# Attention, top-1 experts and a dense softplus layer on one core: the dense layers' rows made gapless in the order of the expert phases, loaded early, and scattered by token at the end

## The chip, the cores and the metric

The kernel runs on one core of a Trainium2 chip. The metric is the device time of one execution in microseconds (us); less is better. Before the change the median of three runs is 951.3 us (951.3, 952.59 and 945.84).

## What is computed

Three layers stand behind one another, all in float32. The reference, cut to what matters:

```python
scores = scale * np.matmul(q, k.transpose(0, 1, 3, 2))          # 4 x 8 x 576 x 576, head size 64
cum = np.cumsum(np.log(np.clip(f, 0.0001, 1.0)), axis=-1)
scores = np.where(causal, -1000000000.0, scores + cum[:, :, :, None] - cum[:, :, None, :])
x = softmax(scores) @ v                                         # as 2304 tokens x 512

expert_idx = np.argmax(logits, axis=1)                          # normed x times normed expert_emb, over tau
gate_w = probs[np.arange(N), expert_idx]                        # softmax over 8 experts
for e in range(E):
    mask = expert_idx == e
    h = np.maximum(x[mask] @ w1[e], 0.0)                        # 512 -> 1024
    out[mask] = gate_w[mask, None] * (h @ w2[e])                # 1024 -> 512

h = x @ w_in                                                    # 512 -> 2048, x is the out above
g = np.maximum(h, 0.0) + np.log1p(np.exp(-np.abs(h)))
return g @ w_out                                                # 2048 -> 512
```

## The kernel before

Float32 products are made of two parts each, a high one (names with h: `xh`, `wh`, `yth`, `gh`) and a low one (`xl`, `wl`, `ytl`, `gl`), and three matmuls: high by high, high by low and low by high. A weight is split by ACT (the high part) and DVE (the difference); both lines are L969 and L970 for the experts' weights and L1251 and L1252 for the dense ones.

The attention fills the first 240 us. It writes x to DRAM (`xd`). Then `route` sorts the tokens by expert into slots of 128 rows; `gidx` holds the token of each row of a slot, `sidx` the row of `yd` to which the result goes: before the change that is the token itself, and for an empty row of a slot a place behind the 2304 real rows.

**Experts.** Nine phases run in the order `ORDER`, each with one expert's weights: phases of kind t take 3 slots, of kind b 2, of kind s 1 (21 slots in all). A phase has four steps that matter here.
- `xgather` (L990): POOL gathers the rows of the phase after the next one from `xd` by `gidx`, one indirect DMA for each slot, into the three buffers `xg`. `xprep` (L1006 to L1008) transposes them on PE and splits them on ACT and DVE.
- The first matmul (L1049) makes h; ACT and DVE take the relu and split it (L1054, L1055). In the one phase of kind s (`small`, phase 6) the operands change places (L1089): ACT writes the relu to `hs` (L1093), PE transposes it (L1099), ACT and DVE split it (L1102, L1103).
- `l2` (L1029) makes y in eight rounds of fb; with three slots a round has 9 matmuls. In the last phase the loop over slots is outside the loop over fb, so the three slots are done one after another.
- `scatter`: ACT evicts y (L1013), and POOL scatters it to `yd` by `sidx` (L1020). y has three buffers.

The loads of raw weights stand on SP. `gates` (L845 to L854) makes the gate of each token behind phase 0. `turn_gates` (L861, L867) turns the gates with two transposes on PE inside the second matmul of phase 1, so that they stand by token in `g.gate`.

**The branch.** Behind the phases a branch (`tc.If(over > 0)`, L1174) jumps over the work for tokens that found no place in the 21 slots. In the profiled execution it jumps. Every engine goes through it.

**Dense layers** (`ffn`). The 18 tiles of 128 rows are taken in five chunks of 4, 3, 4, 3 and 4 tiles. At the start SP loads the four tiles of chunk 0 from `yd` (L1289), DVE multiplies each row by its gate (L1299), PE transposes (L1303), ACT and DVE split (L1304, L1305). For later chunks POOL does the multiplication, and the rest is spread over the units of the chunk before. Each chunk has 16 units of 128 columns of the 2048. Unit n goes through three stations: `l1` on PE (L1316); the softplus, whose parts are ACT's Abs, Exp and two copies (L1325 to L1328) and Ln (L1335), one operation on POOL (L1329), two on DVE (L1340, L1341), and the split into `gh` (ACT, L1344) and `gl` (DVE, L1346); and `l2` (L1358), which PE does three units later. Behind the last unit of a chunk ACT and DVE evict the tiles to `ob` (L1363), and SP stores them to the output (L1365).

The order on each engine is that in which the code issues the instructions; a wait on a semaphore stands ahead of an instruction where its data or its buffer comes from another engine. Instructions behind a waiting one on the same engine wait too. Software DMA queues (DMASW) are those that POOL writes, hardware ones (DMAHW) those of SP and ACT; there are eight semaphores of each.

## Time and profile before

| What | Value |
|---|---|
| median of three runs | 951.3 us |
| lowest, highest | 945.84, 952.59 us |
| profiled execution | 946.24 us |
| its span, from the first to the last instruction | 944.5 us |
| PE busy | 881.7 us (93%), 6294 matmuls |
| DVE, ACT, POOL busy | 618.1, 604.8, 347.0 us |
| mean granted clock of PE | 0.978 |
| share of PE in the chain of waits | 74% |
| DMA | 109.39 MB, mean 116 GB/s |

The profile is of one execution. Its timeline lists instructions by engine with their start and duration; in brackets stands how long the engine was idle before one, and what ended that (for example a DVE instruction of line L864). The chain of waits starts from the last instruction and goes back, at each step to what released it. A duration of a matmul covers its whole way through the pipeline; in a stream the next one starts 0.23 us later.

### The profile page before, as it was taken

Reading aid. Unit: us, or ns where it says so; the run is one execution under the profiler, and the core shown is the slowest. Engines: PE = TensorE matmul, PEld = TensorE weight load, DVE = VectorE, ACT = ScalarE, POOL = GpSimd, SP = SyncE. Lnnn points to the kernel's source line nnn. Section 1 sums busy time; section 2 is a strip of 40 time slices with the busy share of each in tenths; the row PEclk is TensorE's granted clock in tenths of the full one; section 3 lists DMA queues with packets and bytes.
Section 4 is the critical chain, followed back from the end, with each engine's and each line's share of the span. In section 5 each row is a group of like instructions: output and inputs, shape, how many; then the busy total and the mean of one; then the engine's idle time right before and its main releaser. Section 6 shows DMA issues by size and latency. Waiting matters only on the chain.

```text
span 944.5 us, 17382 instructions
## 1 busy us (share of the span) xinstructions
PE 881.7 (93%) x6294; PEld 755.2 (80%) x6294; DVE 618.1 (65%) x1327; ACT 604.8 (64%) x1139; POOL 347.0 (37%) x474
## 2 busy tenths in 40 slices
PE   3999999999299999999999599999999999999998
PEld 2788887878288898897988488889988888988886
DVE  4888888888765777776768476455555455455544
ACT  4778878886624555545444398667676666767664
POOL 6777876774322122122010075323222322222221
PEclk9999999999589999999999799999999999999999
DMA  8766666660337878778853200011001001000001
GB/s 182 177 157 149 163 150 146 166 187 28 113 122 241 300 243 276 231 264 282 281 208 128 82 0 12 12 43 37 23 13 45 11 1 57 23 1 34 1 1 44
DMA packets 103007, 109.39 MB, mean 116 GB/s; under 512 B 62264, under 2 KB 71480, under 8 KB 102912
## 3 DMA queue, kind: packets, MB, share of 16 engines
q1 hardware_dynamic: 99296, 97.02, 35.2%
q0 software_dynamic: 3360, 11.01, 3.3%
q8 instruction: 51, 0.84, 0.4%
q14 instruction: 44, 0.36, 0.1%
q10 hardware_dynamic: 256, 0.16, 0.1%
HBM read 93.15 MB, written 15.02 MB: 115 GB/s over the span
## 4 chain that ended last, share of the span: by engine, by line
PE 74%; DMA 8%; issue 6%; ACT 5%; DVE 5%; POOL 2%; SPq 0%; ACTq 0%; DVEq 0%; POOLq 0%
PE h L1316 21%; PE o L1358 21%; PE h L1049 7%; PE y L1029 5%; DMA yd<-y,sidx 4%; PE s L268 4%; PE av L391 2%; DMA raw<-in_moe_w_dram 2%; PE pt L339 2%; DVE wl L970 2%; PE tps L195 1%; PE av L392 1%; PE av L393 1%; PE s L274 1%; PE s L270 1%
## 5 line engine op out<-in xcount | busy, mean ns | idle before, releaser
L1346 DVE TENSOR_TENSOR gl<-e,gh 128x512 fp32r<-128x512 f32 (+1 forms) x80 | 97.7, 1221 | 170.5 <-ACT gh L1344 170.5
L1329 POOL TENSOR_TENSOR e<-u,e 128x512 f32<-128x512 f32 (+1 forms) x80 | 94.6, 1182 | 281.6 <-ACT u L1328 278.1
L1316 PE MATMUL h<-yth,dl 128*128 128x512 f32 (+1 forms) x320 | 117.9, 369 | 0.0
L1358 PE MATMUL o<-dl,gh 128*128 128x512 f32 x288 | 112.5, 391 | 0.0
L1325 ACT ACTIVATE e<-h 128x512 f32<-128x512 f32 (+1 forms) x80 | 44.4, 554 | 104.0 <-PE h L1316 78.9
L969 ACT ACTIVATE wh<-raw 128x1024 fp32r<-128x1024 f32 x64 | 66.9, 1057 | 49.4 <-DMA raw<-in_moe_w_dram 44.3
L970 DVE TENSOR_TENSOR wl<-raw,wh 128x1024 fp32r<-128x1024 f32 x64 | 77.5, 1221 | 23.4 <-ACT wh L969 22.9
L1049 PE MATMUL h<-xh,wh 128*128 128x384 f32 (+1 forms) x256 | 80.5, 314 | 1.9 <-DVE hl L1055 1.5
L1049 PE MATMUL h<-xh,wl 128*128 128x384 f32 (+1 forms) x256 | 79.6, 311 | 1.5 <-DVE wl L970 1.5
L1049 PE MATMUL h<-xl,wh 128*128 128x384 f32 (+1 forms) x256 | 79.7, 311 | 0.0
L319 DVE SCALAR_TENSOR_TENSOR pts<-pt,pts 128x512 f16<-128x512 f32 (+3 forms) x128 | 69.7, 567 | 11.9 <-ACT pts L316 11.2
L1020 POOL DMA_INDIRECT yd<-y,sidx x21 | 22.2, 1056 | 141.3 <-ACT y L1013 138.2
L316 ACT ACTIVATE pts<-pt 128x512 f16<-128x512 f32 (+3 forms) x128 | 58.4, 495 | 22.1 <-PE pt L329 10.7
L293 ACT ACTIVATE p<-sm,mx 128x512 f32<-128x512 f32 (+3 forms) x128 | 67.8, 558 | 0.0
L1029 PE MATMUL y<-wh,hh 128*128 128x512 f32 x168 | 67.1, 399 | 0.0
L1316 PEld LDWEIGHTS h<-yth,dl 128*128 128x128 f32 x320 | 60.1, 188 | 7.6
L1029 PE MATMUL y<-wl,hh 128*128 128x512 f32 x168 | 66.0, 393 | 0.0
L1341 DVE TENSOR_TENSOR e<-e,v 128x512 f32<-128x512 f32 (+1 forms) x80 | 59.7, 747 | 7.3
L290 DVE CUSTOM_DVE_ANT_0 sm<-s,cb 128x512 f32<-128x512 f32 (+3 forms) x128 | 58.3, 484 | 8.0 <-PE s L270 7.1
L1358 PEld LDWEIGHTS o<-dl,gh 128*128 128x128 f32 x288 | 54.1, 188 | 10.3
L1316 PE MATMUL h<-yth,wh 128*128 128x512 f32 (+1 forms) x160 | 60.4, 378 | 0.7 <-ACT yth L1304 0.7
L391 PE MATMUL av<-vp,pts 128*128 128x65 f16 (+2 forms) x480 | 59.2, 197 | 0.5 <-DVE vbits L240 0.5
(301 smaller groups left out, 2557.2 us busy)
## 6 DMA issues: line engine op xcount, KB each, us to landing
raw<-in_moe_w_dram SPq DMA_DIRECT2D x68, 512.0 KB
cb<-ncum SPq DMA_DIRECT2D x32, 288.0 KB
raw<-in_moe_w_in_dram SPq DMA_DIRECT2D x16, 512.0 KB
raw<-in_moe_w_out_dram SPq DMA_DIRECT2D x16, 512.0 KB
cb<-ncum SPq DMA_DIRECT2D x32, 144.0 KB
out_dram<-ob SPq DMA_DIRECT2D x18, 256.0 KB
qt<-in_q_dram SPq DMA_DIRECT2D x32, 128.0 KB
kt<-in_k_dram SPq DMA_DIRECT2D x32, 128.0 KB
```

Of the source, the lines that this page charges most:

```text
L293: nc.scalar.activation(p[:, 0:n], s[:, 0:n], ACTF.Exp, scale=-1.0, bias=m)
L319: nc.vector.scalar_tensor_tensor(lo, ps, UP, hi, op0=ALU.mult, op1=ALU.subtract)
L391: nc.tensor.matmul(o, ph, vp[0:kk, j, h, 0:D + 1], start=(j == 0), stop=False)
L969: nc.scalar.activation(hi, r, ACTF.Copy)
L970: nc.vector.tensor_sub(lo, r, hi.bitcast(F32))
L1029: nc.tensor.matmul(py[a], x[:, 128 * a:128 * a + 128], w[:, fb % 2], start=(fb == 0 and m == 0 and w is wh), stop=(fb == 7 and m == 1))
L1049: nc.tensor.matmul(pl, x[:, fs], y[:, c], start=(c == 0 and m == 0), stop=(c == 3 and m == 2))
L1316: nc.tensor.matmul(pl, w[:, fs], x[:, d], start=(d == 0 and m == 0), stop=(d == 3 and m == 2))
L1329: nc.gpsimd.tensor_sub(e, u, e)
L1341: nc.vector.tensor_add(d, d, u)
L1346: nc.vector.tensor_sub(gl, d, gh.bitcast(F32))
L1358: nc.tensor.matmul(PO[c][a], x, w, start=(fb == 0 and m == 0 and w is wh), stop=(fb == FB - 1 and m == 1))
```

## The change

**Rows.** `sidx` no longer holds the token. A new `compact` counts, slot by slot in the order of the phases, how many rows of each partition are taken (one matmul with ones, a scan on DVE), and gives the taken rows of `yd` numbers without gaps. So the first 512 rows are results of the first phases. The token travels with the row: `yd` has 528 columns in place of 512, and POOL copies the token's number into the last 16 before the scatter.

**Gates.** `gates` moves into phase 0, behind its first relu. `turn_gates` goes. `store_gates` writes the gates to DRAM (`gd`), POOL gathers them for each slot (`ggather`, 21 more indirect DMAs of one value per row) and the eviction of y multiplies by them (L1078, a scale per row).

**Early load.** In the last phase four tiles are loaded (`rows.load`), transposed and split in rounds fb 2 to 5 (`rows.prep`); the loop over slots is now inside, so that the three scatters come together at the end. The first load is preceded by one of a single element that waits for the scatters issued until then.

**Dense layers.** They keep the pools `xg` and `y` and the PSUM banks of the experts. The multiplication by the gate goes. The first two splits of the second dense weights, which stood ahead of the loop, move into units 0 and 1. The output goes out by POOL, scattered by the token (`oidx`). In the small phase `hs` takes a buffer of the pool `y`.

```diff
-    V.tensor_scalar(pv[:, 0], pid[:, 0], -1.0, 1.0, op0=ALU.mult, op1=ALU.add)
-    V.tensor_tensor(pv[:, 0], pv[:, 0], g.dmf, op=ALU.mult)
-    V.tensor_tensor(g.sidx, g.gidx, pv[:, 0], op=ALU.add)
+    x = 0
+    while x < NMAIN:
...
+        V.tensor_copy(g.flag[:, x:x + y], pid[:, 0, m:m + y])
+        x += y
...
+def store_gates(tc, g, p, ps):
+    nc = tc.nc
+    t = ps()
+    nc.tensor.transpose(t[0:T, 0:128], g.gs, g.ident)
+    turned = p.tile([T, 128], F32, name="turned", bufs=1)
+    nc.vector.tensor_copy(turned, t[0:T, 0:128])
+    nc.scalar.dma_start(g.gd.rearrange("(t p) o -> t (p o)", p=128), turned)
+
+def compact(tc, g, p, ps):
...
+    ones = p.tile([128, 128], BF16, name="ones", bufs=1)
+    nc.gpsimd.memset(ones, 1.0)
+    n = ps()[:, 0:NMAIN]
+    nc.tensor.matmul(n, ones, g.flag, start=True, stop=True)
     yield
+    sums = p.tile([128, NMAIN], F32, name="sums", bufs=1)
+    V.tensor_tensor_scan(sums, ones[:, 0:NMAIN], n, 0.0, op0=ALU.mult, op1=ALU.add)
+    V.tensor_copy(g.total, sums[:, NMAIN - 1:NMAIN])
+    V.tensor_tensor(sums, sums, n, op=ALU.subtract)
+    V.tensor_scalar(sums, sums, g.row, None, op0=ALU.add)
+    V.tensor_tensor(sums, sums, g.dmf, op=ALU.subtract)
+    V.tensor_tensor(sums, sums, g.flag, op=ALU.mult)
+    V.tensor_tensor(g.sidx, sums, g.dmf, op=ALU.add)
+    a = p.tile([128, NMAIN], I32, name="batch", bufs=1)
+    gate_rows(V, g.grow, g.gidx, a)
+    V.tensor_copy(g.tok, g.gidx)
...
+        def ggather(ph):
+            for s in slots(ph):
+                nc.gpsimd.indirect_dma_start(out=g.gsl[:, s:s + 1], out_offset=None, in_=g.gd,
+                                             in_offset=bass.IndirectOffsetOnAxis(ap=g.grow[:, s:s + 1], axis=0))
...
         def scatter(ph, a, py):
-            y = yp.tile([128, DM], F32, name="y", tag="y")
-            nc.scalar.activation(y, py, ACTF.Copy)
...
+            y = yp.tile([128, WROW], F32, name="y", tag="y")
+            nc.gpsimd.tensor_copy(y[:, DM:WROW], tok.to_broadcast([128, WROW - DM]))
+            nc.scalar.activation(y[:, 0:DM], py, ACTF.Copy, scale=gate)
...
+            if last:
+                for a in range(SIZES[0]):
+                    rows.load(0, a)
+            if ph == 0:
+                store_gates(tc, g, hp, bank)
...
-                if ph == 1 and i in (5, 6):
-                    next(turned, None)
...
+                if fb == 1:
+                    ggather(ph)
...
-                if last and i % 3 == 1:
-                    conv.split("i", i // 6, i // 3 % 2)
-                if fb == 7:
-                    for a in rows:
-                        scatter(ph, a, py[a])
+                if last:
+                    conv.split("i", fb // 2, fb % 2)
+                    if 2 <= fb < 2 + SIZES[0]:
+                        rows.prep(0, fb - 2, bank)
+            for a in range(w):
+                scatter(ph, a, py[a])
...
-                hs = hp.tile([128, 512], F32, name="hs", tag="hs", bufs=2)
+                hs = yp.tile([128, WROW], F32, name="hs", tag="y")[:, 0:DM]
...
+    def load(self, c, a):
+        g, t = self.g, FIRST[c] + a
+        y = self.y[t] = g.xp.tile([128, WROW], F32, name="yg", tag="xg", bufs=3)
+        if t == 0:
+            self.nc.sync.dma_start(y[0:1, 0:1], g.yd[0:1, 0:1])
+        self.nc.sync.dma_start(y, (g.yd if c else g.ydv[NSLOT])[128 * t:128 * t + 128])
+
+    def prep(self, c, a, bank):
...
+        nc.gpsimd.tensor_copy(g.oidx[:, t:t + 1], y[:, DM:DM + 1])
+        p = bank().rearrange("p (d n) -> p d n", n=128)
+        for d in range(4):
+            nc.tensor.transpose(p[:, d], y[:, 128 * d:128 * d + 128], g.ident)
+        nc.scalar.activation(hi[:, :, a], p, ACTF.Copy)
+        nc.vector.tensor_sub(lo[:, :, a], p, hi[:, :, a].bitcast(F32))
...
-                    r = 128 * (FIRST[c] + a)
-                    nc.sync.dma_start(out[r:r + 128, :], o)
+                    t = FIRST[c] + a
+                    nc.gpsimd.indirect_dma_start(out=outv[t], out_offset=bass.IndirectOffsetOnAxis(ap=g.oidx[:, t:t + 1], axis=0),
+                                                 in_=o, in_offset=None)
...
-        for a in range(SIZES[0]):
-            yload(0, a)
-        for pair in range(2):
-            conv.split("o", 0, pair)
-        late = iter([(q, pair) for q in range(1, 4) for pair in range(2)])
...
+        late = iter([(q, pair) for q in range(4) for pair in range(2)])
...
-                        conv.split("o", q, pair, nc.gpsimd)
+            for q, pair in [next(late, (0, None))]:
+                if pair is not None:
+                    conv.split("o", q, pair, nc.gpsimd if q else nc.vector)
```

The order of the program shows three places. The first is ACT behind the branch, before: the two splits of dense weights, the four splits of transposed rows, and unit 0's softplus up to `gh`, the high part of its result.

```order
L1174 UNCONDITIONAL_BRANCH [waits Activation_49,Activation_sequencer_49]
L1251 ACTIVATE wh<-dw 128x1024 [waits DVE_49,PE_49,Activation_49]
L1251 ACTIVATE wl<-dw 128x1024
L1304 ACTIVATE yth_12338<-yt 128x4x128 [waits PE_49] x4
L1325 ACTIVATE e<-h 128x512 [waits DMASW4_49,DMASW2_49,DMASW6_49,DMASW0_49,PE_49]
L1326 ACTIVATE e<-e 128x512 [waits Activation_49]
L1327 ACTIVATE u<-e 128x512 [waits DMASW2_49,DMASW1_49,DMASW6_49,DMASW0_49,Activation_49]
L1328 ACTIVATE u<-u 128x512 [waits Activation_49]
L1335 ACTIVATE v<-u 128x512 [waits Activation_49]
```

And the same place after the change (the lines have moved: L1396 is Abs, L1351 the split of weights, L1415 the copy to `gh`).

```order
L1396 ACTIVATE e<-h 128x512 [waits DMASW5_49,DMASW6_49,DMASW4_49,DMASW7_49,DMASW3_49,DMAHW0_49,DMASW1_49,DMAHW3_49,DMASW0_49,DMAHW7_49,PE_49,Pool_49]
L1397 ACTIVATE e<-e 128x512 [waits Activation_49]
L1398 ACTIVATE u<-e 128x512 [waits Activation_49,Pool_49]
L1399 ACTIVATE u<-u 128x512 [waits Activation_49]
L1351 ACTIVATE wh<-dw 128x1024 [waits DVE_49]
L1406 ACTIVATE v<-u 128x512 [waits DMASW3_49,DMASW4_49,DMASW2_49,DMASW5_49,DMASW1_49,DMASW6_49,DMASW0_49,DMASW7_49,Activation_49,Pool_49]
L1396 ACTIVATE e<-h 128x512 [waits DMAHW2_49,DMASW2_49,PE_49]
L1397 ACTIVATE e<-e 128x512 [waits Activation_49]
L1398 ACTIVATE u<-e 128x512 [waits DMASW7_49,Activation_49]
L1399 ACTIVATE u<-u 128x512 [waits Activation_49]
L1415 ACTIVATE gh<-e 128x512 [waits DVE_49]
L1351 ACTIVATE wl<-dw 128x1024
```

The two splits ahead of the dense layers and the four of the rows have gone from here; one split of weights stands inside unit 0 and one behind `gh`. Unit 0's Abs now has all eight software queues but one in its list of waits.

The second place is ACT at the small phase, before: the last evictions of the phase ahead of it, its relu (`hs`) and the splits of weights (`wh`) around it.

```order
L1013 ACTIVATE y<-y 128x512 [waits DMASW0_49,PE_49,Activation_49]
L1013 ACTIVATE y<-y 128x512 [waits DMASW1_49,PE_49,Activation_49]
L1093 ACTIVATE hs<-h 128x512 [waits PE_49]
L969 ACTIVATE wh<-raw 128x1024 [waits DMAHW6_49,DVE_49]
L969 ACTIVATE wh<-raw 128x1024 [waits DMAHW7_49,DVE_49]
L1102 ACTIVATE hh<-ht 128x512 [waits PE_49]
L969 ACTIVATE wh<-raw 128x1024 [waits DMAHW0_49,DVE_49]
```

And after the change (L1078 is the eviction, L1161 the relu).

```order
L1078 ACTIVATE y<-y,gsl 128x512 [waits DMASW1_49,PE_49,DMASW3_49,Activation_49,Pool_49]
L1078 ACTIVATE y<-y,gsl 128x512 [waits DMASW2_49,PE_49,DMASW4_49,Activation_49,Pool_49]
L1161 ACTIVATE hs<-h 128x512 [waits PE_49,DMASW3_49,Activation_49,Pool_49]
L1017 ACTIVATE wh<-raw 128x1024 [waits DMAHW7_49,DVE_49]
L1017 ACTIVATE wh<-raw 128x1024 [waits DMAHW0_49,DVE_49]
L1170 ACTIVATE hh<-t 128x512 [waits PE_49]
L1017 ACTIVATE wh<-raw 128x1024 [waits DMAHW1_49,DVE_49]
```

The order is the same; the relu waits for a software queue, ACT and POOL beside PE, since it takes the buffer of a scattered y.

The third place is POOL at the program's end, before: its operation of the softplus (`e<-u,e`) in the last units.

```order
L1299 TENSOR_SCALAR yg<-yg,gate 128x512 [waits DMAHW1_49,PE_49,Pool_49]
L1329 TENSOR_TENSOR e<-u,e 128x384 [waits DVE_49,Activation_49] x3
L1299 TENSOR_SCALAR yg<-yg,gate 128x512 [waits DMAHW2_49,PE_49,Pool_49]
L1329 TENSOR_TENSOR e<-u,e 128x384 [waits DVE_49,Activation_49] x5
L1329 TENSOR_TENSOR e<-u,e 128x512 [waits DVE_49,Activation_49] x16
L1435 UNCONDITIONAL_BRANCH
```

And after the change (L1400 is the same operation).

```order
L1400 TENSOR_TENSOR e<-u,e 128x384 [waits DVE_49,Activation_49] x3
L1400 TENSOR_TENSOR e<-u,e 128x512 [waits DVE_49,Activation_49] x3
L1437 DMA out_dram<-ob,oidx 2304x512 [waits DMASW2_49,Activation_49]
L1437 DMA out_dram<-ob,oidx 2304x512 [waits DMASW3_49,DVE_49]
L1437 DMA out_dram<-ob,oidx 2304x512 [waits DMASW4_49,Activation_49]
L1400 TENSOR_TENSOR e<-u,e 128x512 [waits Activation_49] x2
L1400 TENSOR_TENSOR e<-u,e 128x512 [waits DVE_49,Activation_49] x11
L1437 DMA out_dram<-ob,oidx 2304x512 [waits DMASW5_49,Activation_49]
L1437 DMA out_dram<-ob,oidx 2304x512 [waits DMASW6_49,DVE_49]
L1437 DMA out_dram<-ob,oidx 2304x512 [waits DMASW7_49,Activation_49]
L1437 DMA out_dram<-ob,oidx 2304x512 [waits DMASW0_49,DVE_49]
L1495 UNCONDITIONAL_BRANCH
```

The stores of the output, which stood on SP, have moved to POOL, behind its work for the chunk and ahead of that for the next one.

## Rows read from the trace of the kernel before

**Rows 1.** The chain of waits: start us, us, what

```profile
529.61 3.39 DMA y<-yd
...
538.80 10.95 PE h L1316 x47
...
549.75 2.72 PE o L1358 x12
...
929.43 10.89 PE o L1358 x48
```

**Rows 2.** Busy by stretch: length; PE, PEld, DVE, ACT, POOL; clock, DMA share, GB/s

```profile
265.00:300.00 35.00, 35.00 (x175) 31.97 (x176) 22.64 (x34) 8.51 (x14) 3.43 (x7) 0.96 0.52 171
524.00:552.50 28.50, 17.85 (x77) 14.73 (x78) 12.55 (x15) 15.26 (x24) 6.59 (x5) 0.82 0.17 58
700.00:942.00 242.00, 240.31 (x1115) 203.99 (x1113) 124.55 (x155) 161.70 (x295) 63.60 (x54) 1.00 0.06 21
```

**Rows 3.** Timeline of PE: start, us, what, [idle before]

```profile
523.42 0.39 PE L1029 MATMUL y<-wh,hl 128*128 128x512 f32 x1
...
538.08 0.50 PE L1316 MATMUL h<-yth,wh 128*128 128x512 f32 x1 [0.69 <-ACT yth L1304]
```

**Rows 4.** Timeline of SP, the first dense rows

```profile
529.61 1.89 SPq L1289 DMA_DIRECT2D y<-yd  x4
```

**Rows 5.** Timeline of PE, transposes inside the first expert phase

```profile
285.09 1.03 PE L1006 MATMUL xt<-ident,xg 128*128 128x128 f32 x8
...
285.88 0.47 PE L1029 MATMUL y<-wh,hh 128*128 128x512 f32 x1
```

**Rows 6.** Timeline of ACT, from the branch to the first dense unit

```profile
526.99 1.06 ACT L1251 ACTIVATE wh<-dw 128x1024 fp32r<-128x1024 f32 x1 [2.50 <-ACTq L1174]
...
541.63 0.60 ACT L1325 ACTIVATE e<-h 128x512 f32<-128x512 f32 x1 [3.61 <-PE h L1316]
...
547.27 0.61 ACT L1344 ACTIVATE gh<-e 128x512 fp32r<-128x512 f32 x1
```

**Rows 7.** Groups of ACT by line and shape: mean ns

```profile
L443 ACT ACTIVATE xr<-xt,vs 128x512 f32<-128x512 f32 x15 | 10.1, 673 | 0.0
```

**Rows 8.** Timeline of POOL, gathers and the scatters of the last two phases

```profile
255.88 1.86 POOL L990 DMA_INDIRECT xg<-xd,gidx  x1 [6.49 <-ACT wh L1195]
...
260.05 0.95 POOL L990 DMA_INDIRECT xg<-xd,gidx  x1 [0.30 <-issue]
...
491.59 0.97 POOL L1020 DMA_INDIRECT yd<-y,sidx  x1 [0.31 <-issue]
...
524.77 0.97 POOL L1020 DMA_INDIRECT yd<-y,sidx  x1 [4.47 <-ACT y L1013]
```

**Rows 9.** Timeline of PE behind the first gather

```profile
260.13 1.11 PE L1006 MATMUL xt<-ident,xg 128*128 128x128 f32 x4 [5.59 <-DMA xg<-xd,gidx]
```

**Rows 10.** Timeline of DVE, beside the gathers and in the passage

```profile
255.43 4.62 DVE L732 TENSOR_TENSOR wl<-raw,wh 128x1024 fp32r<-128x1024 f32 x4
...
528.08 1.23 DVE L1252 TENSOR_TENSOR dl<-dw,wh 128x1024 fp32r<-128x1024 f32 x1 [4.16 <-ACT wh L1251]
...
547.92 1.37 DVE L1346 TENSOR_TENSOR gl<-e,gh 128x512 fp32r<-128x512 f32 x1 [0.79 <-ACT gh L1344]
```

**Rows 11.** Timeline of PE in phase 1

```profile
326.17 0.20 PE L867 MATMUL gt<-ident,turned 20*128 20x20 f32 x1 [2.11 <-DVE turned L864]
```

**Rows 12.** Timeline of POOL and ACT around the small phase

```profile
435.17 0.99 POOL L1020 DMA_INDIRECT yd<-y,sidx  x1 [13.55 <-ACT y L1013]
...
437.46 0.60 ACT L1093 ACTIVATE hs<-h 128x512 f32<-128x512 f32 x1 [1.60 <-PE h L1089]
```

**Rows 13.** Timeline at the end: POOL, SP, DVE

```profile
926.75 1.29 POOL L1329 TENSOR_TENSOR e<-u,e 128x512 f32<-128x512 f32 x1 [4.15 <-ACT u L1328]
...
938.92 2.48 SPq L1365 DMA_DIRECT2D out_dram<-ob  x4
...
940.35 0.69 DVE L1363 COPY ob<-o 128x512 f32<-128x512 f32 x1 [0.67 <-PE o L1358]
```

More of the change, by code (lines that the diff above doesn't have):

```diff
@@ L45 @@
 NSLOT = len(SLOTS)
+PLACES = [(k, j, a) for k, j in ORDER for a in range(WIDTH[k])]
+SB = 640
+WROW = 528
+SIZES = [4, 3, 4, 3, 4]
+FIRST = [sum(SIZES[:c]) for c in range(len(SIZES))]
 @with_exitstack
@@ L1059, in wide @@
                         conv.step()
+                    if ph == 0 and (gg, a) == (0, 0):
+                        gates(tc, g)
+                    if ph == 0 and gg < 2 and a:
+                        next(places, None)
                 hts += [(hh[:, a], hl[:, a]) for a in range(2)]
                 feed(ph, 0)
+            if last:
[3 more added lines that the diff above has]
+                store_gates(tc, g, hp, bank)
             py = [ps_y.tile([128, DM], F32, name="y", tag="y") for _ in range(w)]
-            for i, (rows, fb) in enumerate([([a], fb) for a in range(w) for fb in range(8)] if last else
-                                           [(list(range(w)), fb) for fb in range(8)]):
-                l2(ph, py, hts[fb], fb, rows)
-                if i == 0:
+            for fb in range(8):
+                l2(ph, py, hts[fb], fb, range(w))
+                if fb == 0:
                     xprep(ph + 1)
@@ L1096, in turn @@
             def turn(hs):
-                t = ps_t.tile([128, 4, 128], F32, name="ht", tag="T")
+                t = bank().rearrange("p (c n) -> p c n", n=128)
                 for c in range(4):
@@ L1201, in experts @@
             wsplit(0, c)
-        turned = turn_gates(tc, g, hp, ps_t)
+        rows = Rows(tc, g)
+        places = compact(tc, g, hp, bank)
         for ph in range(n_ph):
@@ L1256, in get, with ffn @@
         return self.hi[kind, q][d // 2][:, s], self.lo[kind, q, d // 2][:, s]
-def ffn(tc, g, conv, out):
+def ffn(tc, g, conv, rows, out):
     nc = tc.nc
-    ident, yd, gate = g.ident, g.yd, g.gate
     FB = F2 // 128
-    SIZES = [4, 3, 4, 3, 4]
-    FIRST = [sum(SIZES[:c]) for c in range(len(SIZES))]
     NC = len(SIZES)
+    outv = dram_disjoint_views(out, N // 128)
     with ExitStack() as ctx:
@@ L1310, in l1 @@
             fs = slice(128 * (fb % 4), 128 * (fb % 4) + 128)
-            yh, yl = (t.rearrange("p c a n -> p c (a n)") for t in yT[c])
+            yh, yl = (t.rearrange("p c a n -> p c (a n)") for t in rows.turned[c])
             pl = ps_h.tile([128, 128 * SIZES[c]], F32, name="h", tag="h")
@@ L1350, in l2 @@
             if fb == 0:
-                PO[c] = [ps_o.tile([128, DM], F32, name="o", tag="o") for _ in range(SIZES[c])]
+                PO[c] = [ps_o.tile([128, DM], F32, name="y", tag="y") if a < 3 else
+                         ps_t.tile([128, DM], F32, name="t", tag="U") for a in range(SIZES[c])]
             gh, gl = G.pop((c, fb))
@@ L1399, in ffn @@
                     if fb == x + 3 * a:
-                        yload(c + 1, a)
-                    if fb == x + 1 + 3 * a:
-                        turn = yprep(c + 1, a)
-                        next(turn)
+                        rows.load(c + 1, a)
                     if fb == x + 2 + 3 * a:
-                        next(turn, None)
+                        rows.prep(c + 1, a, bank)
 _INS = ["q", "k", "v", "f", "moe_expert_emb", "moe_tau", "moe_w1", "moe_w2", "moe2_w_in", "moe2_w_out"]
```

191 lines of the change are left out of this document (94 added, 97 removed).

## The prediction, made before the changed kernel had run

> **What bounds the kernel now.** I read four views in this order: the chain of waits, the busy times by stretch, the timeline of the engines where the chain leaves PE, and the order of the changed program. The chain ends in PE's matmuls of the dense layers, and the dense part is filled by PE: 240.31 of 242 us between 700 and 942 [rows 1, 2]. The first expert phase is filled too, 35.00 of 35 us [rows 2]. So a change to the other engines pays only where PE waits. The largest such place after the attention is the passage from the experts to the dense layers: there the chain goes over a scatter, the load of the rows and their transposes [rows 1], and in 28.5 us PE works 17.85 [rows 2]. PE's last expert matmul starts at 523.42 and is through at 523.65 (0.23 us each in the stream); its first dense matmul starts at 538.08, a gap of 14.4 us [rows 3]. The first unit of the second dense matmul is through at 549.75 + 2.72 = 552.47 [rows 1]: 28.8 us after 523.65, and that is the figure to compare, since four units of the first matmul and one of the second must be done by then in either kernel.
>
> **The passage, step by step.** Removed from it: the load of the first rows (SP at 529.61, data 3.39 us later), their scaling, the transposes and the split on ACT and DVE [rows 1, 3, 4]. They go into the last expert phase, where PE does the 16 transposes between its matmuls. Eight of them cost PE 0.79 us (285.09 to 285.88 [rows 5]), so 16 cost 1.6, with a short pause 1.8 us. The loads come in time: they wait for scatters of phases that are long done, and the fourth, which waits for a buffer, is issued three rounds (9 matmuls, 2.04 us each, so 6.1 us) before its transposes, against 3.39 us from issue to data.
>
> The branch over the overflow work stays: ACT's first work behind it comes 2.50 us after its last [rows 6]. So the first dense matmul can start some 2.7 us after the last expert one, and the first three units of 12 matmuls end at 2.7 + 3 x 2.72 = 10.9. What is late next is the softplus of unit 0. In the changed order its first ACT instruction (Abs) waits for the software DMA queues, the three last scatters among them. Before, these scatters left one by one, the last 4.47 us after POOL's work before it [rows 8]; now all three come at the end. Evictions of 0.67 us (a form with a scale per row [rows 7]) and POOL's 0.97 us + 0.30 between two [rows 8] put POOL's last end at 4.4 to 4.7 us after PE's. Landing after that: at least 2.39 us by the gather (POOL done 257.74, PE starts 260.13 [rows 8, 9]), at most 3.87 by the last scatter (POOL done 525.74, the load that waits for it 529.61 [rows 4, 8]), in which the branch may hide. I take the upper one, since it is a scatter: Abs starts at 8.5 us (6.8 to 10.1, the upper with writing slowed).
>
> From Abs of unit 0 to the end of its second matmul: before, gh starts 547.27 - 541.63 = 5.64 us after Abs [rows 6]. The change puts the first two splits of the second dense weights, done in the gap before, into units 0 and 1: one ACT split of 1.06 us ahead of gh, so gh ends at 7.3; one more ACT split (8.3), DVE's own half of it, 1.23 us (9.6), then gl, 1.37 us, at 10.95 [rows 6, 10]; the last four matmuls, 0.23 each, end at 11.9. The first unit of the second matmul is through at 8.5 + 11.9 = 20.4 us. The passage gains 28.8 - 1.8 - 20.4 = **6.6 us** (5.0 to 8.3). About half of the old wait comes back as a wait for the scatters.
>
> **The other parts.**
> - Phase 1: the two transposes that turn the gates, and PE's wait of 2.11 us for DVE between them, go [rows 11]. Nothing else is late there. -2.0 us (-2.4 to -0.5).
> - Small phase: its relu writes into the pool of the scattered rows and waits until the scatter of three tiles before has landed. That scatter ends on POOL at 436.16, lands 2.4 to 3.87 us later, and the relu stood at 437.46 [rows 12]: 1.1 to 2.6 us late. Queued behind it on ACT are weight splits, on PE the transposes of its result, which the chain runs through. +1.7 us (0.3 to 2.6; the low end if PE's later waits there swallow it).
> - End: four stores went out on SP, issued between 938.92 and 941.40, the last eviction ending at 941.04, and the span ended at 944.5 [rows 13], 3.4 us after it. Now POOL writes each store: from 938.92 with a pitch of 1.28 us the fourth starts at 942.76 and ends at 943.7; with the same landing as above, 946.1 to 947.6. +2.5 us (1.6 to 3.1).
> - Phase 0: the gates' arithmetic, the sum over flags and one more matmul come in. ACT is busy 8.51 and DVE 22.64 of 35 us there [rows 2], so three bank buffers hide most. +0.3 (0 to 1.0). If that cover failed, PE would stand as long as ACT needs for the gates, about 3 us.
> - Middle of the dense layers: the row scaling on POOL goes, four or three stores by POOL at each of four chunk edges come in. Four take 5.1 us; POOL idles 4.15 us before each of its units [rows 13], and PE asks for that unit's result three units later. 0 (-1 to +2). Gate gathers and 16 extra columns per row (3%) lie beside PE-bound work: 0.
>
> **Sum** on the profiled execution, 946.24 us (span 944.5): -6.6 - 2.0 + 1.7 + 2.5 + 0.3 = -4.1, so 942.1. The median of three runs is 951.3, with 945.84 the lowest: on that base it is 947.2. I take 945. All good ends together give -9.8, all bad ones +3.2.
>
> **A rule weighed.** Beside DVE's 4.62 us of tensor operations a gather takes POOL 1.86 us, and one as DVE ends 0.95 [rows 8, 10]. The Trainium skill, "SBUF — State Buffer", "Who interferes with whom", says that descriptors written by POOL starve only while DVE is in a two-port mode, which a tensor_tensor does not have; the trace shows a stretch beside tensor_tensor, so I do not count on that exemption. The same page ("A bandwidth-pool intuition that's wrong") gives some 0.62 us alone against 3.1 overlapped: at 2.1 us more for each of the seven below the sum would be an estimated +11. Neither is needed below.
>
> **Rivals.**
> 1. The whole wait goes. If the scatters land before the Abs is ready (5.4 us after PE's end, when unit 0 of the first matmul is through), the second matmul's first unit is through at 5.4 + 11.9 = 17.3, the passage gains 9.7, and with -2.0 in phase 1, +0.3 in the small phase +1.6 at the end and +0.3 in phase 0 the sum is -9.5: 936.7 us. For it: nothing in unit 0's data needs these scatters. Against it: the order names the wait, and POOL's three writings alone end at 4.4.
> 2. POOL's writing becomes the bound (slower). Seven instructions of POOL now stand one after another on the chain: three last scatters and four last stores. If each takes not 0.97 but 1.86 us, as the first gather beside DVE [rows 8], that is 7 x 0.89 = 6.2 us more, so -4.1 + 6.2 = +2.1: 948.3 us. It decides from 0.59 us more for each; over 1% slower from 1.95 more. For it: rows 8. Against it: at both places DVE has little to do.
> 3. The gain is hidden: the fourth load comes late by one load's 3.39 us [rows 1], and PE waits for it at the transposes inside the last phase. Then the passage gains 3.2 and the sum is -0.7: 945.5 us. For it: four loads share three buffers. Against it: 6.1 us of lead against 3.39.
> 4. The change doesn't do what it says: rows of the first four tiles would be among the last scatters, and the early load had to wait for them. The order shows that it waits only for earlier ones, and rows in phase order put the first 512 into the first phases.
>
> **How the numbers follow.** Forecast 0.58; rival 1 0.20; rival 2 0.13; rival 3 0.08; rival 4 0.01. Over 1% (9.5 us, about what a measurement of this kernel can tell from no change) faster: rival 1, which lies at that bound, and the good end of the forecast, 0.22. Slower by over 1%: rival 2 at its far end, or a wait that I do not see, 0.10. Within 1%: 0.68. The range goes from rival 1 on the profiled base (936) to the bad ends on the base of the median (955).
>
> **What would show it.** Right: a gap on PE of about 2.7 us behind the last expert matmul, three units of the first dense matmul, then a pause of some 6 us; unit 0's Abs starting when the third last scatter lands; no wait for the turned gates; the small phase's relu released by a DMA, not by PE; the last store leaving POOL 2.7 us after the last eviction has ended. Wrong: an Abs without a wait, PE waiting at the transposes inside the last phase, POOL's stores near 2 us, or PE waiting at chunk edges.

## The result, and the profile after

The changed kernel takes 958.53 us (median of 9 runs, 956.48 to 960.67) against 951.23 us before (9 runs, 945.84 to 954.95): a ratio of 1.0082, 95% interval [1.0059, 1.0105]. It is slower by 0.8%, where 945 us, a gain, had been forecast.

The profiled execution of the changed kernel took 957.64 us, its span 955.9, so 11.4 us more than the 944.5 of before. The two spans are compared at four marks on PE: the first transpose of gathered rows, the end of the last expert matmul, the end of the first unit of the second dense matmul, and the end of the last matmul. An end is taken 0.23 us behind the start of the last matmul.

| Stretch | before | after | difference |
|---|---|---|---|
| to the first transpose of gathered rows | 260.13 | 262.32 | +2.2 |
| experts, to the end of the last matmul | 263.5 | 265.0 | +1.5 |
| passage, to the end of the first unit of the second dense matmul | 28.7 | 22.5 | -6.2 |
| dense layers, to the end of the last matmul | 387.8 | 394.7 | +6.8 |
| end of the span | 4.4 | 11.4 | +7.1 |

The first line need not be the change's: the kernel before, profiled a second time with its tiles moved (e2 below), stands at 262.72 there. So the change costs some 9 us in these two executions, and two stretches make it, the dense layers and the end. The passage did become shorter. The medians lie only 7.3 us apart: the profiled execution of before, 946.24 us, lies 5.0 us below its median, that of after 0.9 us. e2, at 951.94 us, needs 31.1 us for the passage, with the granted clock at its lower level for 17.1 us there in place of 10.2; beside e2 the change wins 8.6 us in the passage and not 6.2, and loses 6.9 and 7.1 us behind it.

**The passage.** PE's timeline of the changed kernel:

```profile
526.63 0.86 PE L1088 MATMUL y<-wh,hl 128*128 128x512 f32 x3
...
530.28 0.51 PE L1387 MATMUL h<-yth,wh 128*128 128x512 f32 x1 [2.78 <-ACTq L1246]
...
542.61 0.79 PE L1387 MATMUL h<-yth,wh 128*128 128x512 f32 x1 [3.66 <-DVE e L1411]
...
547.00 0.40 PE L1430 MATMUL y<-wh,gh 128*128 128x512 f32 x1
```

The matmul that ends the experts is the third of the first row, through at 527.33. The first dense matmul starts 2.95 us later, behind the branch; the gap of 14.4 us of [rows 3] is gone. Three units follow, and then PE waits 3.66 us for DVE, ahead of the fourth. ACT shows why:

```profile
527.19 1.84 ACT L1078 ACTIVATE y<-y,gsl 128x512 f32<-128x512 f32 x3 [1.36 <-issue]
...
536.87 0.60 ACT L1396 ACTIVATE e<-h 128x512 f32<-128x512 f32 x1 [7.84 <-DMA yd<-y,sidx]
...
543.39 0.63 ACT L1415 ACTIVATE gh<-e 128x512 fp32r<-128x512 f32 x1
```

Abs of unit 0 stood idle for 7.84 us, released by the scatter (`yd<-y,sidx`). It starts at 536.87, 9.5 us after the last expert matmul. POOL wrote the three scatters one after another:

```profile
528.65 1.01 POOL L1079 DMA_INDIRECT yd<-y,sidx  x1 [9.60 <-ACT y L1078]
...
530.15 0.98 POOL L1079 DMA_INDIRECT yd<-y,sidx  x1 [0.28 <-POOL y L1077]
...
531.63 0.98 POOL L1079 DMA_INDIRECT yd<-y,sidx  x1 [0.28 <-POOL y L1077]
```

The last is through at 532.61, 5.3 us after PE's end; 1.49 us lie between two starts, since a copy of the token stands ahead of each (with one scatter of [rows 8] it was 1.28). Landing takes 4.3 us more. Behind Abs the chain runs to DVE, whose first operation on unit 0 frees the bank of PSUM that PE's fourth unit needs:

```profile
541.88 0.68 DVE L1411 SCALAR_TENSOR_TENSOR e<-h,e 128x512 f32<-128x512 f32 x1
...
546.14 0.68 DVE L1417 TENSOR_TENSOR gl<-e,gh 128x512 fp32r<-128x512 f32 x1
```

It ends at 542.56, PE goes on at 542.61. By then PE had stood for 3.7 us, and the granted clock is at the lower of its two levels (a row of busy times by stretch: length, then busy time of PE, PEld, DVE, ACT and POOL, then the clock):

```profile
542.61:546.00 3.39, 3.39 (x8) 2.71 (x9) 1.70 (x2) 3.33 (x6) 1.28 (x1) 0.51 0.00 0
546.00:550.00 4.00, 4.00 (x18) 3.24 (x18) 3.20 (x6) 3.64 (x6) 1.42 (x2) 1.00 0.00 0
```

At 0.51 of 2.4 GHz eight matmuls take 3.4 us in place of 1.9. The second unit's end comes at 549.79, 22.5 us after the experts.

**The dense layers.** PE is as full as before, 20.00 us of busy time in each stretch of 20 us from 560 to 940, but with fewer matmuls in most of them. One such stretch, after and then before:

```profile
700.00:720.00 20.00, 20.00 (x90) 16.19 (x89) 12.10 (x14) 14.25 (x26) 8.06 (x8) 1.00 0.15 53
```

```profile
700.00:720.00 20.00, 20.00 (x92) 16.55 (x91) 11.93 (x14) 14.75 (x27) 7.40 (x6) 1.00 0.15 52
```

What is longer is each matmul. Two units at the same place of the last chunk, after:

```profile
885.89 0.39 PE L1387 MATMUL h<-yth,wh 128*128 128x512 f32 x1
...
886.12 0.39 PE L1387 MATMUL h<-ytl,wh 128*128 128x512 f32 x1
...
886.35 0.39 PE L1387 MATMUL h<-yth,dl 128*128 128x512 f32 x1
...
891.47 0.39 PE L1387 MATMUL h<-yth,wh 128*128 128x512 f32 x1
```

and before:

```profile
872.15 0.39 PE L1316 MATMUL h<-yth,wh 128*128 128x512 f32 x1
...
872.38 0.39 PE L1316 MATMUL h<-ytl,wh 128*128 128x512 f32 x1
...
872.60 0.39 PE L1316 MATMUL h<-yth,dl 128*128 128x512 f32 x1
...
877.59 0.39 PE L1316 MATMUL h<-yth,wh 128*128 128x512 f32 x1
```

From one unit's first row to the next unit's there are 24 matmuls: 5.58 us after, 5.44 us before, so 0.2325 and 0.2267 us for one. No wait stands between them, the clock is 1.00 in both.

**The end.** POOL and DVE after, with the first and the last store:

```profile
943.44 0.99 POOL L1437 DMA_INDIRECT out_dram<-ob,oidx  x1 [5.96 <-ACT ob L1435]
...
947.27 0.96 POOL L1437 DMA_INDIRECT out_dram<-ob,oidx  x1 [0.30 <-issue]
...
944.66 0.69 DVE L1435 COPY ob<-t 128x512 f32<-128x512 f32 x1 [0.69 <-PE t L1430]
```

and the busy times by stretch behind it (the last two columns are the share of the DMA engines and GB/s):

```profile
946.00:948.00 2.00, 0.00 (x0) 0.00 (x0) 0.00 (x0) 0.00 (x0) 1.69 (x2) 1.00 0.55 227
948.00:950.00 2.00, 0.00 (x0) 0.00 (x0) 0.00 (x0) 0.00 (x0) 0.23 (x1) 0.67 0.41 166
950.00:952.00 2.00, 0.00 (x0) 0.00 (x0) 0.00 (x0) 0.00 (x0) 0.00 (x0) 0.50 0.00 0
952.00:954.00 2.00, 0.00 (x0) 0.00 (x0) 0.00 (x0) 0.00 (x0) 0.00 (x0) 0.50 0.00 0
```

The last eviction ends at 945.35; POOL is through with the last store at 948.23, the DMA engines are done before 950, and the span ends at 955.9. Before, the last eviction of [rows 13] was followed by 3.4 us, with the DMA engines done before 943:

```profile
942.00:943.00 1.00, 0.00 (x0) 0.00 (x0) 0.00 (x0) 0.00 (x0) 0.00 (x0) 1.00 0.65 244
943.00:944.00 1.00, 0.00 (x0) 0.00 (x0) 0.00 (x0) 0.00 (x0) 0.00 (x0) 0.76 0.00 0
```

**Experts.** The wait for the turned gates [rows 11] is gone. The small phase's relu does wait for the scatter, 2.55 us of idle ACT, and PE 0.54 us for it:

```profile
438.21 0.60 ACT L1161 ACTIVATE hs<-h 128x512 f32<-128x512 f32 x1 [2.55 <-DMA yd<-y,sidx]
...
438.86 0.65 PE L1167 MATMUL t<-ident,hs 128*128 128x128 f32 x4 [0.54 <-ACT hs L1161]
```

In phase 5 a split of weights waits for its load longer than before, and PE behind it:

```profile
411.83 1.06 ACT L1017 ACTIVATE wh<-raw 128x1024 fp32r<-128x1024 f32 x1 [4.38 <-DMA raw<-in_moe_w_dram]
...
414.68 0.44 PE L1108 MATMUL h<-xh,wh 128*128 128x384 f32 x1 [1.47 <-DVE hl L1114]
```

Before, the same wait of ACT was 2.81 us and PE did not wait:

```profile
412.68 1.06 ACT L969 ACTIVATE wh<-raw 128x1024 fp32r<-128x1024 f32 x1 [2.81 <-DMA raw<-in_moe_w_dram]
```

PE reached phase 5 136.1 us after its first transpose (398.37 - 262.32), before 140.7 (400.84 - 260.13). What it won ahead of that, it partly waits for the weights, here and once more in phase 7 (0.88 and 0.64 us at 454 to 456). From its first matmul to that of the next phase the small phase took 17.6 us, in e2 16.2; in the profiled execution of before it took 17.7, but there the granted clock was 0.50 for 3.4 us of it.

### The profile page after: what moved, and what is told of

It is laid out like the page before. It is cut to its first block, busy times and chain, and to the rows that moved or that the text cites. A ratio compares the mean times of both kernels' runs of the same rounds, so it can differ in the third digit from the quotient of the medians.

```text
span 955.9 us, 17466 instructions
## 1 busy us (share of the span) xinstructions
PE 889.6 (93%) x6294; PEld 753.5 (79%) x6294; DVE 617.6 (65%) x1332; ACT 606.5 (63%) x1139; POOL 391.6 (41%) x539
## 4 chain that ended last, share of the span: by engine, by line
PE 68%; issue 10%; DMA 6%; DVE 5%; ACT 5%; POOL 3%; SPq 0%; POOLq 0%; ACTq 0%; DVEq 0%
PE h L1387 17%; PE y L1430 14%; PE y L1088 9%; PE h L1108 6%; DMA raw<-in_moe_w_dram 4%; PE s L279 4%; PE t L1430 2%; PE av L402 2%; PE pt L350 2%; POOL e L1400 2%; DVE wl L1018 2%; PE tps L206 2%; ACT wh L1017 1%; PE av L403 1%; PE av L404 1%
## 5 line engine op out<-in xcount | busy, mean ns | idle before, releaser
L1400 POOL TENSOR_TENSOR e<-u,e 128x512 f32<-128x512 f32 (+1 forms) x80 | 95.0, 1187 | 267.7 <-ACT u L1399 226.9
L1396 ACT ACTIVATE e<-h 128x512 f32<-128x512 f32 (+1 forms) x80 | 44.3, 554 | 119.7 <-PE h L1387 94.8
L1018 DVE TENSOR_TENSOR wl<-raw,wh 128x1024 fp32r<-128x1024 f32 x64 | 77.7, 1224 | 28.7 <-ACT wh L1017 28.7
L1430 PE MATMUL y<-dl,gh 128*128 128x512 f32 x240 | 94.4, 393 | 0.0
L1387 PE MATMUL h<-ytl,wh 128*128 128x512 f32 (+1 forms) x160 | 59.9, 374 | 0.0
L1387 PE MATMUL h<-yth,wl 128*128 128x512 f32 (+1 forms) x160 | 59.7, 373 | 0.0
```

The costliest lines, as they stand in the source:

```text
L1018: nc.vector.tensor_sub(lo, r, hi.bitcast(F32))
L1387: nc.tensor.matmul(pl, w[:, fs], x[:, d], start=(d == 0 and m == 0), stop=(d == 3 and m == 2))
L1400: nc.gpsimd.tensor_sub(e, u, e)
L1430: nc.tensor.matmul(PO[c][a], x, w, start=(fb == 0 and m == 0 and w is wh), stop=(fb == FB - 1 and m == 1))
```

## The experiments

**Theories after the result.** For the pace of the matmuls: (A) it depends on where the two operands of a matmul lie in the partition of SBUF, which the new tiles have moved; rival (B): it comes from the new order or from POOL's DMAs. For the end: (C) stores on a queue that POOL writes are slow to complete; rival: something else that is left to drain. For the passage: (D) the shared buffers make Abs wait; rival: a further wait behind it. Where tiles lie stands in the built program, not in the profile. The starts modulo 512 B, and the mean time from the start of one matmul to that of the next in us, over all pairs of equal size from the same line that follow each other within 0.3 us at the full clock:

```
                 start of  weights rows hidden   512 columns, dense   256 columns,
                                                  first    second     experts
before                       384   384   384      0.2271   0.2282     0.1211
changed                      256   448   128      0.2331   0.2323     0.1159
e1 equal starts              384   384   384      0.2274   0.2282     0.1210
e2 before, moved             448   448   448      0.2271   0.2282     0.1209
e5 changed, moved            384    64   256      0.2331   0.2323     0.1162
e6 hidden tiles apart        384   384   128      0.2272   0.2283     0.1211
e10 other distances          256   384   320      0.2329   0.2327     0.1196
e11 hidden tiles off         384   384   256      0.2296   0.2328     0.1204
e12 rows off                 384    64   384      0.2333   0.2294     0.1168
e9 best                      256   256   256      0.2273   0.2283     0.1207
```

The rows are the transposed inputs (`xh`, `xl`, `yth`, `ytl` of four tiles), the hidden tiles `hh`, `hl`, `gh`, `gl`. The first matmul of a layer reads weights and rows, the second one hidden tiles and weights. A distance is counted here from the weights to the other operand.

**e1: the changed kernel, operands at equal starts**

```diff
+    const.tile([128, 32], F32, name="padc")
     g.flag = const.tile([128, NMAIN], BF16, name="flag")
...
         xp = g.xp = pool("e_x", 1)
+        xp.tile([128, 80], F32, name="padx", tag="padx")
         yp = g.yp = pool("e_y", 3)
+        yp.tile([128, 80], F32, name="pady", tag="pady", bufs=1)
```

> The changed kernel with three unused tiles (128 B behind the constants, 320 B ahead of the gathered rows, 320 B ahead of the scattered rows of each partition), so that every operand of PE starts at 384 B modulo 512 in its partition, as in the kernel before (in the changed kernel the weights start at 256, the transposed rows at 448, the hidden tiles at 128). Nothing that is computed or waited for changes. Theory A (where the operands lie sets the pace of a matmul): a 512-column matmul starts every 0.2267 us again, not every 0.2325, the dense part from the first to the last second matmul takes 388 us, not 395.4, and the time falls by 7 to 10 us. Theory B (the pace comes from the order or from more software DMA): the pace stays 0.2325 and the time within 1 us of the changed kernel's 958.5.

Measured: the pace is back (table), the dense part takes 388.3 us, and the ratio to the kernel before is 1.0020 [0.9999, 1.0040] (10 runs, median 952.18) in place of 1.0082. Unused tiles alone give back 6 us: theory A holds, B falls, and the sum's largest error is shown. Two units of the last chunk stand 5.44 us apart again (24 matmuls of 0.2267 us):

```profile
886.50 0.39 PE L1390 MATMUL h<-yth,wh 128*128 128x512 f32 x1
...
891.94 0.39 PE L1390 MATMUL h<-yth,wh 128*128 128x512 f32 x1
```

Its profiled execution was the slowest of the ten; in it the experts took 272.4 us.

**e2: the kernel before, all operands moved by 64 B**

```diff
+    const.tile([128, 16], F32, name="padc")
     g.gate = const.tile([128, N // 128], F32, name="gate")
```

> The kernel before with one unused tile of 64 B behind the constants, so that all of PE's operands start at 448 B modulo 512 in place of 384. Theory A with the start itself as what counts: the 512-column pace changes from 0.2267 us, and by up to 0.006. Theory A with only the distance between a matmul's two operands counting (it stays 0 modulo 512): the pace stays 0.2267. Theory B: it stays 0.2267 as well.

Measured: 0.2271, as before, dense part 387.8 us, 951.94 us in one run. The start itself does not count.

**e5: the changed kernel, all operands moved by 128 B**

```diff
+    const.tile([128, 32], F32, name="padc")
     g.flag = const.tile([128, NMAIN], BF16, name="flag")
```

> The changed kernel with 128 B of unused tile behind the constants: every start moves by 128 B (weights at 384 modulo 512, transposed rows at 64, hidden tiles at 256), every distance between two operands stays as in the changed kernel (192 and 128 modulo 512). If the distance of a matmul's two operands sets the pace, 512 columns stay at 0.2325 us and 256 columns at 0.116. If the start of the weights itself does (384 as in the kernel before), 512 columns go back to 0.227.

Measured: 0.2331, 0.2323, and 0.1162 for 256 columns, 957.48 us. With the weights back at 384 nothing has changed: not the weights' start, but the distance counts.

**e6: rows with the weights, hidden tiles 256 B away**

```diff
-        yp.tile([128, 80], F32, name="pady", tag="pady", bufs=1)
+        yp.tile([128, 16], F32, name="pady", tag="pady", bufs=1)
```

(against e1)

> As e1_place, but the hidden tiles stay 256 B modulo 512 away from the weights (starts: weights and transposed rows 384, hidden tiles 128). If each matmul's own two operands count, the first matmuls of both layers (weights by rows) keep e1's pace, 0.227 in the dense first matmul and 0.121 for 256 columns, and the second ones (hidden tiles by weights) differ from it, up to 0.2325. If only the rows count, all stay at 0.227; if any odd placement slows every matmul, all go to 0.2325.

Measured: both stay fast, 0.2272 and 0.2283; 955.12 us. That is what was expected if only the rows count, but a distance of 256 B that is as good as none gives it too. e10 to e12 decide.

**e10: rows 128 B and hidden tiles 64 B from the weights**

```diff
         xp = g.xp = pool("e_x", 1)
+        xp.tile([128, 112], F32, name="padx", tag="padx")
         yp = g.yp = pool("e_y", 3)
+        yp.tile([128, 64], F32, name="pady", tag="pady", bufs=1)
```

> The changed kernel with unused tiles such that the rows start 128 B (modulo 512) from the weights and the hidden tiles 64 B. If the distance of a matmul's two operands modulo 256 B sets its pace, the dense first matmul (rows) keeps the slow pace, 0.2325 us for 512 columns, as the second one had at a distance of 128 in the changed kernel; the second one shows what 64 B makes: 0.2325 if every distance that is no multiple of 256 B is slow, 0.227 if only some are. If it were the start of the weights (256) that slows, all would stay at 0.2325.

Measured: 0.2329 and 0.2327, 962.4 us. With 64 B the second matmul is as slow as with 128. In e9 the weights start at 256, as here, and all is fast: it is not the weights' start.

**e11 and e12: only the hidden tiles off, only the rows off**

```diff
-        yp.tile([128, 80], F32, name="pady", tag="pady", bufs=1)
+        yp.tile([128, 48], F32, name="pady", tag="pady", bufs=1)
```

(e11, against e1; in e12 the tile `padx` has 128 columns and `pady` 32)

> As e1_place, but the hidden tiles start 128 B (modulo 256) from the weights, and the rows at the same place as the weights. If each matmul's own two operands count, the second matmuls (hidden tiles by weights) are slow, 0.231 to 0.232 us for 512 columns in both layers, and the first ones stay fast, 0.227, with 0.121 for 256 columns. If only the rows count, all stay at 0.227.

> As e1_place, but the rows start 192 B (modulo 256) from the weights, as in the changed kernel, and the hidden tiles at the same place as the weights. If each matmul's own two operands count, the dense first matmul is slow for 512 columns (0.233) and the experts' first one faster for 256 columns (0.116), while the second matmuls stay fast at 0.227. If the rows set the pace of all, the second ones are slow as well.

Measured: with the hidden tiles off, the second matmuls are slow (0.2328, in the experts 0.2323) and 256 columns stay at 0.1204; with the rows off, the first one is slow (0.2333), 256 columns take 0.1168, and the experts' second stays at 0.2277. Each matmul's own two operands count, and so it was the 256 B that made e6 fast. In the dense part, where the two kinds follow each other unit by unit, the other kind is touched as well, by some 0.001 to 0.0025 us (0.2296 for the first in e11, 0.2294 for the second in e12); why is not shown. The dense part takes 393.7 and 392.3 us, the runs 960.61 and 953.47.

**e3: the output stored by SP**

```diff
-                    nc.gpsimd.indirect_dma_start(out=outv[t], out_offset=bass.IndirectOffsetOnAxis(ap=g.oidx[:, t:t + 1], axis=0),
-                                                 in_=o, in_offset=None)
+                    nc.sync.dma_start(out[128 * t:128 * t + 128, :], o)
```

> The changed kernel with the output stored by SP in the order of the rows, without the scatter by token (so the rows of the output stand in the order of the phases). Theory C (the stores by POOL cost the end): from the end of the last eviction to the end of the span 3.4 us as before the change, not 10.5, and the time is 6 to 7 us less. Rival (the end is long for another reason, such as the drain of the software queues used earlier): 8 to 10 us stay. The pace of the matmuls stays 0.2325 by theory A and B, and falls to 0.2267 if POOL's stores slowed PE.

Measured: 950.86 us in one run; the end takes 4.24 us in place of 11.43, and the dense part 394.69 (394.68 in the changed kernel): stores by POOL at the chunk edges had cost PE nothing, stores at the end 7.2 us. SP and DVE at the end of e3:

```profile
943.59 2.52 SPq L1437 DMA_DIRECT2D out_dram<-ob  x4
...
945.06 0.69 DVE L1435 COPY ob<-t 128x512 f32<-128x512 f32 x1 [0.69 <-PE t L1430]
```

The last eviction ends at 945.75 and the span at 949.1, 3.4 us later, as before the change.

**e7: the same plain stores, issued by POOL**

```diff
-                    nc.sync.dma_start(out[128 * t:128 * t + 128, :], o)
+                    nc.gpsimd.dma_start(out[128 * t:128 * t + 128, :], o)
```

(against e3)

> As e3_end_sp (output in the order of the rows, no scatter by token), but the plain stores are issued by POOL. Theory C1 (a software queue's completion costs the end, whatever it writes): from the last dense matmul to the end of the span 9 to 11.4 us, as with the scatter. Theory C2 (the scatter by rows costs it): 4.3 to 6 us, near SP's 4.24.

Measured: 9.27 us, 955.55 us in one run. Of the 7.2 us, some 5 come with POOL as the issuer, some 2 with the scatter. POOL is through at 946.16 and the DMA engines are done before 948; the span ends at 953.7:

```profile
945.62 0.54 POOL L1437 DMA_DIRECT2D out_dram<-ob  x1 [0.25 <-DVE ob L1435]
```

```profile
946.00:948.00 2.00, 0.00 (x0) 0.00 (x0) 0.00 (x0) 0.00 (x0) 0.15 (x1) 1.00 0.65 262
948.00:950.00 2.00, 0.00 (x0) 0.00 (x0) 0.00 (x0) 0.00 (x0) 0.00 (x0) 0.66 0.00 0
950.00:953.70 3.70, 0.00 (x0) 0.00 (x0) 0.00 (x0) 0.00 (x0) 0.00 (x0) 0.50 0.00 0
```

So some 6 us pass without data, where SP's stores need some 1.7 (before the change their last data end at 942.76, the span at 944.45). POOL's queue does not cost this where SP writes the last stores: in e9 POOL's last scatter is written at 860.83, 77 us before the end, and the end takes 4.0 us. What happens in those 6 us no row shows. A scatter in the passage takes some 2.6 us from the last data to its release: in the changed kernel the data of the scatters end at 534.3, and Abs starts at 536.87.

```profile
533.00:534.00 1.00, 1.00 (x6) 0.81 (x5) 0.00 (x0) 0.00 (x0) 0.00 (x0) 1.00 0.72 279
534.00:536.00 2.00, 2.00 (x11) 1.58 (x10) 0.00 (x0) 0.00 (x0) 0.00 (x0) 1.00 0.02 6
```

**e4: unit 0's softplus tiles apart**

```diff
-            e = wide(g.xp, "e", "xg", bufs=3)[:, 0:n]
-            u = wide(g.yp, "u", "y")[:, 0:n]
+            if (c, fb) == (0, 0):
+                e = gp.tile([128, n], F32, name="e0", tag="gh")
+                u = gp.tile([128, n], F32, name="u0", tag="gh")
+            else:
+                e = wide(g.xp, "e", "xg", bufs=3)[:, 0:n]
+                u = wide(g.yp, "u", "y")[:, 0:n]
```

(and `v` likewise in a buffer of `gl`)

> The changed kernel with the softplus tiles of the first dense unit (e, u, v) in buffers of the hidden tiles, which no scatter reads. Theory D (the first Abs waits for the last scatters because of the shared buffers): Abs starts some 5.8 us after the last expert matmul in place of 9.5, and the first unit of the second dense matmul is through 3 to 4 us earlier, at 18.5 to 19.5 in place of 22.5 us. Rival (another wait stands behind it, such as the software queues of the branch): Abs stays at 9 to 9.5 us.

Measured: Abs is released by PE, 6.0 us after the last expert matmul (530.68); PE waits 1.17 us in place of 3.66, at the full clock, and the mark comes at 18.5 us, not 22.5. Theory D holds. The run as a whole took 957.04 us; its experts took 268.1, 3.1 more than the changed kernel's.

```profile
536.73 0.60 ACT L1400 ACTIVATE e<-h 128x512 f32<-128x512 f32 x1 [4.34 <-PE h L1387]
...
543.46 0.50 PE L1387 MATMUL h<-yth,wh 128*128 128x512 f32 x1 [1.17 <-DVE e L1418]
```

**e8: the three together**

```diff
+    V.tensor_scalar(g.own, g.ptok, float(128 * FIRST[-1]), None, op0=ALU.is_ge)
+    V.tensor_tensor(g.own, g.own, g.flag, op=ALU.mult)
+    V.tensor_tensor(g.few, g.flag, g.own, op=ALU.subtract)
     n = ps()[:, 0:NMAIN]
-    nc.tensor.matmul(n, ones, g.flag, start=True, stop=True)
+    nc.tensor.matmul(n, ones, g.few, start=True, stop=True)
...
+                    if c == NC - 1:
+                        nc.sync.dma_start(outv[t][128 * t:128 * t + 128], o)
+                        continue
```

(beside e4's edit and unused tiles; tokens from 1792 on keep their own row, so the last chunk needs no scatter)

> The changed kernel with three things together: operands at equal distance (256 modulo 512 all), unit 0's softplus tiles in buffers of the hidden tiles, and the last chunk kept by token (tokens from 1792 on keep their own row, the others stand gapless ahead of them), so that SP stores the last four tiles. If the three terms add (6.3 us of pace, 4 us in the passage, 7.1 us at the end), the time is 958.5 - 17.4 = 941 us, ratio 0.989 to the kernel before. If the gains do not add (the weight stream takes back what PE wins in the experts, or the first unit's chain only moves), 945 to 950 us.

Measured: 950.18 us (10 runs), ratio 0.9992 [0.9974, 1.0011]. Passage 19.0, dense part 388.3 and end 4.1 came as expected; but the experts took 273.9 us, 8.9 more than the changed kernel's. Of these 5.9 are one wait: the matmul over the flags now stood behind more work of DVE, in the middle of phase 0:

```profile
279.24 0.18 PE L904 MATMUL t<-few,ones 128*128 128x21 bf16 x1 [5.91 <-DVE few L902]
```

**e9: the same, with that wait mended**

```diff
+    nc.gpsimd.tensor_scalar(g.own, g.ptok, float(128 * FIRST[-1]), 0.0, op0=ALU.is_ge, op1=ALU.add)
...
+    yield
     n = ps()[:, 0:NMAIN]
...
+        for pair in range(2):
+            conv.split("o", 0, pair)
+        late = iter([(q, pair) for q in range(1, 4) for pair in range(2)])
```

> As e8_best, with two mends: the flags of the tokens that keep their row are made on POOL and PE's matmul over them is issued two units later (in e8 PE waited 5.9 us for DVE there), and the first two splits of the second dense weights stand ahead of the dense units again, as in the kernel before. If the three terms add: the experts (from the first transposes to the last matmul) take 264 to 266 us in place of e8's 273.9, the first unit of the second dense matmul is through 17 us after the last expert matmul (e8: 19.0), and the time is 939 to 943 us, ratio 0.988 to 0.992. If the weight stream takes it back: the experts stay over 268 us and the time is 945 to 948 us.

Measured: 941.43 us (4 runs, 939.8 to 941.97) against 950.73; ratio 0.9902 [0.9886, 0.9919]: faster than the kernel before by about 1%, and below the changed one's 958.53 by 1.8%. Experts 267.0 (264 to 266 expected), passage 17.3, dense part 388.4, end 4.0 us. ACT and PE in its passage:

```profile
534.66 0.60 ACT L1427 ACTIVATE e<-h 128x512 f32<-128x512 f32 x1 [0.88 <-PE h L1414]
...
541.02 0.62 ACT L1449 ACTIVATE gh<-e 128x512 fp32r<-128x512 f32 x1
...
531.59 0.50 PE L1414 MATMUL h<-yth,wh 128*128 128x512 f32 x1 [3.10 <-ACTq L1272]
...
542.88 0.39 PE L1464 MATMUL y<-wh,gh 128*128 128x512 f32 x1
```

PE starts behind the branch and then has no wait that the timeline shows up to the second matmul: four units of 12 times 0.227 us, 10.9 us, fill nearly all of the 11.3 us to it.

## Why the prediction was wrong

- **The step that failed most: "Middle of the dense layers", put at "0 (-1 to +2)".** I looked for waits, of POOL and at chunk edges, and there are none (e3). The 6.8 us come from the matmuls themselves, 1380 of 512 columns at some 0.005 us each. The wider tiles of 528 columns and a few small ones moved the operands, so that two operands of a matmul no longer start at the same place modulo 256 B. Shown by e1, e2, e11 and e12. I had taken the matmul's 0.23 us as a constant.
- **The end: +2.5 us (1.6 to 3.1) forecast, +7.1 measured.** POOL's pitch was right (1.27 us, last store through 2.9 us after the last eviction). Wrong was "with the same landing as above": the 2.39 to 3.87 us came from DMAs in the middle of the program; at its end the same kind of queue takes 7.7 us. e3 and e7 show that it is POOL's queue.
- **The passage: -6.6 us with the transposes (which fall into the experts' stretch), so 20.4 us to the mark, measured 22.5.** The mechanism was right: the branch, three units, a wait for the scatters, and Abs behind the third of them. Mis-sized were the scatters, 9.5 us in place of 8.5, as the copies of the token lie between them and the landing takes 4.3 us; and PE, which I let run at full clock behind its pause, got 0.51 for 3.4 us (1.5 us). My chain over gl wasn't the last; the bank for the fourth unit was.
- **Phase 1, small phase, phase 0 and transposes: +1.8 - 2.0 + 1.7 + 0.3 = +1.8 forecast for the experts, +1.5 measured.** That the sum agrees is luck; its terms agree only in part. The gates' wait is gone, and the transposes cost about 1.8 (starts 2.53 us apart where a round takes 2.09). In the small phase PE's waits grew by 0.9 us, and beside e2 the phase got 1.4 us longer; 1.7 were forecast. Part of what phase 1 gained was taken back in phases 5 and 7, where PE now waits for weights. The moved operands, in no term of the forecast, count here too, and nearly cancel: 504 matmuls of 512 columns took 0.2323 us in place of 0.2278 (some +2.3 us), 384 of 256 columns 0.1159 in place of 0.1211 (some -2.0). Nine other executions with the change's order put the experts at 264.7 to 272.4 us, against 263.5 and 264.2 before, the longer ones with longer waits for DVE's split of the relu; how much of that is the change's is open.
- **Rivals.** Rival 1 was a real saving, but only when made (e4, e9). Rival 2 named the right instructions, POOL's, and the wrong price: their writing took 0.96 to 1.01 us each; what was slow at the end is what follows. Rivals 3 and 4 did not occur: no row shows PE waiting for the transposes in the last phase.

Together: forecast -4.1; +6.8 from the pace, +4.6 at the end and +2.1 in the passage give +9.4, and 11.4 less the 2.2 us ahead of the experts is 9.2. That account is of the two profiled executions; the medians, 7.3 us apart, were not taken apart in this way.

## What to carry to other kernels

A change that adds or widens a tile moves every tile behind it, and a loop that PE fills can change its pace by up to 2.6% (5.58 against 5.44 us for a unit here) without any new wait: compare the time from the start of one matmul to that of the next, between equal matmuls, before reading any waits. Price the last store of a kernel by a row of a last store on that queue, not by a landing in the middle. And a shared buffer saves space at the price of a wait for its last reader; at a stage's edge that reader may be a DMA.

## What the runs showed that was not expected

- The pace of these matmuls follows the distance between the starts of their two operands in the partition: at 0 B modulo 512, and at 256 B with the hidden tiles (e6), 0.227 to 0.228 us for 512 columns; with 64, 128 or 192 B modulo 256, 0.232 to 0.233. For 256 columns it is the other way round: 0.116 to 0.117 us with rows 192 B from the weights, 0.1196 at 128, 0.121 at 0. Why is not shown.
- Stores of a program's last tiles cost 4.2 us from the last matmul on SP, 9.3 on POOL with plain rows, 11.4 scattered.
